# A polysketch attention and feed-forward kernel: the order of its steps behind the sixtieth, and who runs some of them

## The chip, the core and the metric

The kernel runs on one core of a Trainium2 chip. The metric is the device time of one execution in microseconds (us). The core's engines are TensorE (PE, the matmuls, with its weight loads PEld), VectorE (DVE), ScalarE (ACT), GpSimd (POOL) and SyncE (SP, which issues most of the transfers). Each runs its own instructions in the order of the program and waits for the others on semaphores.

## The reference

```python
{'batch': 4, 'n_heads': 4, 'seq': 1088, 'head_dim': 32}; r = 8
def phi(x):
    a = np.einsum('rd,bhsd->bhsr', S1, x)
    b = np.einsum('rd,bhsd->bhsr', S2, x)
    return np.einsum('bhsi,bhsj->bhsij', a, b).reshape(*x.shape[:-1], r * r)
q_p, k_p = phi(q), phi(k)
kv = np.einsum('bhsf,bhsd->bhfd', k_p, v)
z = np.sum(k_p, axis=2)
num = np.einsum('bhsf,bhfd->bhsd', q_p, kv)
den = np.einsum('bhsf,bhf->bhs', q_p, z)[..., None] + 1e-06
attn_out = num / den
x = attn_out.transpose(0, 2, 1, 3).reshape(4352, 128)
h = ((x @ w1) * (x @ w2)) @ w3        # w1, w2: 128 x 1024, w3: 1024 x 1024
out = h @ w_out                       # w_out: 1024 x 128
```

Linear attention with a feature map of 64 products a token, and then a feed-forward block in which two projections are multiplied. All inputs and the output are float32.

## The kernel before

The work is cut into some 1,700 named steps. The part ahead of the dot says of what: `k0` to `k3` and `q0` to `q6`, `qr` are the keys and queries of the attention by batch or chunk, `s` the sketch matrices, `w0` to `w10` pieces of the weights, `f` the products of w3 with w_out, `g0` to `g7` the feed-forward block for 512 tokens each, `gr` the same for the last 256 tokens, `h4` and `h6` a shared form for the groups g4/g5 and g6/g7 that makes two groups from seven products (`P1` to `P7`) of sums. The part behind the dot is the operation: `load` a transfer in, `gram` the 32-wide products of a key chunk with itself (line 659), `T` and `N` small products that build the sketch's coordinates (lines 883 to 912), `kv` the sums over keys (line 769), `x` the attention output (lines 1297, 1527), `a`, `b` (lines 1799, 1809) the two projections, `m` their product, `o` the output product (1824, 1835), `P` the output product of the shared form (1759), `k1` to `k9` the additions that build the two groups from the products (lines 1771 to 1785), `oT` the transposition of an output block, `oS` a scaling of it on POOL or DVE (1848), `st` its store (1556, 1562). A step `.a0` or `.a1` of a weight (line 470) adds the two halves of split weight words; `.c`, `.m`, `.j` (lines 263, 462, 466) come ahead of it.

The constants `zeros`, `ident` and masks come first. `ORDER` is one list of all steps; every engine runs its own instructions in the order in which the list has them. `SLOTS` is one string for each kind of buffer: which buffer the n-th user gets. The set `POOL` names the steps whose additions run on POOL and not on DVE, `CPV` and `CPG` the copies that run on DVE and on POOL and not on ACT. A step waits, through semaphores, for what it reads and for the buffer it writes. `WARM` gives the number of idle matmuls (line 255) in the steps `warm0` to `warm11`: they keep TensorE busy at the start and compute nothing that is used. The transfers of weights and of q, k, v are issued on SP in the order of the list, each only when the fourth before it has landed:

```python
WARM = [27, 2, 3, 4, 4, 4, 1, 2, 1, 1, 2, 2]
UNDER_WAY = 4
for ins, ahead in zip(bulk[UNDER_WAY:], bulk):
```

A matmul's weight tile has rows and columns, and its shape differs by step: 128 by 128 in `a`, `b`, `o`, 128 by 64 in `P`, 64 by 128 in the sums ahead of them (line 1673), 128 by 32 in `gram` and `kv`, 32 by 32 in `N` and the later `x`.

## Time and profile before

| what | us |
|---|---|
| median of three runs (lowest, highest) | 245.12 (245.04, 245.3) |
| the profiled execution, first to last instruction (its span) | 244.1 |
| the median above that span | 1.0 |
| TensorE matmuls, busy | 236.2 |
| DVE, busy | 206.7 |
| POOL, busy | 161.9 |
| ACT, busy | 123.5 |
| mean granted TensorE clock | 0.998 |

The profiled execution's own time is its span, and what lies around it before and behind is in the runs' times and not in the span. The first feed-forward product starts at 27.42 us; the last matmul ends at 240.57; the last store is issued at 240.95. "Issue" among the waits is time in which an engine waited for nothing that the profile shows.

### The profile page before, as it was taken

How to read it: one execution, taken by the hardware profiler on the slowest of the kernel's cores; microseconds unless marked ns; L12 is line 12 of the kernel's file. 1: busy time of each engine (PE TensorE's matmuls, PEld its weight loads, DVE VectorE, ACT ScalarE, POOL GpSimd, SP SyncE). 2: the span in 40 equal slices, each digit the busy share in tenths (PEclk: the TensorE clock that was granted, in tenths of full speed). 3: DMA queues.
4: the chain of work that ended last, by engine and by line, in shares of the span. 5: the costliest groups of instructions: out<-in, count | busy, mean ns of one | idle time of the engine just before them, and what ended most of it. 6: DMA issues, size and time to landing. Idle time of an engine off the chain costs nothing.

```text
span 244.1 us, 6745 instructions
## 1 busy us (share of the span) xinstructions
PE 236.2 (97%) x2724; PEld 129.8 (53%) x2724; DVE 206.7 (85%) x421; ACT 123.5 (51%) x246; POOL 161.9 (66%) x203
## 2 busy tenths in 40 slices
PE   8998999899999999999999999999999999999994
...
PEclk9999999999999999999999999999999999999999
...
GB/s 201 265 143 325 181 227 190 6 197 224 220 141 251 188 217 190 59 1 3 3 0 0 4 0 3 59 113 3 1 0 0 0 3 0 0 1 3 12 90 93
DMA packets 31935, 22.06 MB, mean 90 GB/s; under 512 B 21280, under 2 KB 26528, under 8 KB 31904
## 3 DMA queue, kind: packets, MB, share of 16 engines
...
q8 instruction: 21, 0.34, 0.6%
...
## 4 chain that ended last, share of the span: by engine, by line
PE 87%; DMA 5%; ACT 2%; POOL 2%; DVE 1%; issue 1%; POOLq 0%; SPq 0%
PE b_ps L1809 12%; PE ps_o L1835 12%; PE ps_X L1673 11%; PE a_ps L1799 11%; PE ps_o L1759 10%; PE ps_w3o L534 6%; PE ps_Y L1673 6%; PE ps_Z L1673 3%; PE ps_g L659 2%; PE ps_x L1527 2%; PE ps_ac L1374 2%; DMA qh<-in_q_dram 2%; DMA k<-in_k_dram 2%; PE ps_or L1824 2%; POOL ph L1208 1%; PE idle_ps L255 1%
## 5 line engine op out<-in xcount | busy, mean ns | idle before, releaser
L1673 PE MATMUL ps_X<-xd,wv 64*128 64x512 f32 x112 | 36.3, 593 | 0.0
L1799 PE MATMUL a_ps<-xT,w 128*128 128x512 f32 (+1 forms) x80 | 36.1, 562 | 0.0
L1809 PE MATMUL b_ps<-xT,w 128*128 128x512 f32 (+1 forms) x80 | 35.6, 555 | 0.0
L1804 ACT COPY ffa<-a_ps 128x512 f32<-128x512 f32 (+1 forms) x38 | 20.1, 540 | 29.2 <-PE a_ps L1799 26.7
L1707 POOL TENSOR_TENSOR hc<-hc 128x512 f32<-128x512 f32 x16 | 20.7, 1304 | 15.7 <-DVE hc L1685 15.5
L1835 PE MATMUL ps_o<-ab,w3o 128*128 128x512 f32 x64 | 29.6, 600 | 0.0
L1680 ACT COPY hc<-ps_X 128x512 f32<-128x512 f32 x38 | 21.3, 590 | 16.1 <-PE ps_X L1673 12.9
L1815 DVE TENSOR_TENSOR ab<-ffa,b_ps 128x512 f32<-128x512 f32 (+1 forms) x40 | 23.9, 623 | 4.9 <-PE b_ps L1809 4.1
L501 POOL TENSOR_TENSOR w3c<-w3c,cv_m 128x512 int32<-128x512 int32 x16 | 21.2, 1344 | 4.2 <-DVE w3c L495 4.1
L1673 PEld LDWEIGHTS ps_X<-xd,wv 64*128 64x128 f32 x112 | 14.9, 186 | 13.1 <-issue 10.9
L1799 PEld LDWEIGHTS a_ps<-xT,w 128*128 128x128 f32 x80 | 14.1, 189 | 13.9 <-issue 8.8
L1809 PEld LDWEIGHTS b_ps<-xT,w 128*128 128x128 f32 x80 | 14.4, 190 | 13.1 <-issue 8.1
L1673 PE MATMUL ps_Y<-xd,wv 64*128 64x512 f32 x48 | 19.7, 594 | 0.0
L1835 PEld LDWEIGHTS ps_o<-ab,w3o 128*128 128x128 f32 x64 | 11.6, 190 | 13.4 <-issue 13.0
L534 PEld LDWEIGHTS ps_w3o<-wo,w3T 128*128 128x128 f32 x128 | 15.3, 192 | 2.4 <-issue 2.4
L534 PE MATMUL ps_w3o<-wo,w3T 128*128 128x128 f32 x128 | 15.7, 276 | 0.0
L1759 PE MATMUL ps_o<-hc,w3o 128*64 128x512 f32 x32 | 15.1, 595 | 0.0
L1759 PE MATMUL ps_o<-tt,ws 128*64 128x512 f32 x32 | 13.7, 594 | 0.0
L1680 ACT COPY hc<-ps_Y 128x512 f32<-128x512 f32 x14 | 8.1, 592 | 9.7 <-PE ps_Y L1673 6.6
L263 ACT ACTIVATE cv_c<-raw 128x1024 f32<-128x1024 f32 (+1 forms) x13 | 13.0, 1014 | 0.0
L1540 ACT COPY xd<-ps_x 64x256 f32<-64x256 f32 x24 | 8.8, 367 | 7.2 <-PE ps_o L1835 6.8
...
## 6 DMA issues: line engine op xcount, KB each, us to landing
...
```

Of the source, the lines that this page charges most:

```text
L263: act.activation(dst, hi.bitcast(F32), ACT.Prelu, scale=2.0 ** -112, alpha=-2.0 ** 32)
L501: pool.tensor_tensor(d, d, x["m"][:, i * 512:(i + 1) * 512], ALU.add)
L534: pe.matmul(t["o"], w3T[ko][:, c], wo[:, c], start=c == 0, stop=c == NC - 1)
L1673: pe.matmul(x[bank], stat(j, u)[:, i * 128:(i + 1) * 128], rows(j, u), start=new, stop=True, tile_position=(u * 64, 0), skip_group_check=True)
L1680: cp(n(y))(x[k], x[bank])
L1707: on(f"h{g}.{i}m{k}").tensor_mul(both[0][k], both[0][k], both[1][k])
L1759: pe.matmul(acc_o[bank][half[0]:half[1]], w(i), x(i), start=n == 1, stop=n == (2 if j == 3 else 4), tile_position=(0, half[0]), skip_group ...
L1799: pe.matmul(x["a"][:, :w], w_of(0, c), xT[g][:, c0:c0 + w], start=True, stop=True)
L1804: cp(f"g{g}.{c}{su}c")(x["s"][:, :w], x["a"][:, :w])
L1809: pe.matmul(x["b"][:, :w], w_of(1, c), xT[g][:, c0:c0 + w], start=True, stop=True)
L1815: dve.tensor_mul(ab_sb[g, c][:, c0:c0 + w], x["s"][:, :w], x["b"][:, :w])
L1835: pe.matmul(o_ps[g], w3o[:, c], ab_sb[g, c], start=n == 1, stop=n == NC)
```

## The change

The instructions are the same, and the first 60 steps of the list stay. Behind them `ORDER` is another list of the same steps. With it the buffers in `SLOTS` change, and the engine of some steps: TensorTensor instructions on DVE are 189 instead of 201 and on POOL 143 instead of 131, copies on ACT 168 instead of 173 and on DVE 26 instead of 21. `WARM` is the same, but `warm8`, `warm9` and `warm11` stand elsewhere in the list.

```diff
 POOL = set("""
-    g4.oS g5.oS g6.oS g7.oS h4.0T1 h4.0T2 h4.0T3 h4.0m12 h4.0m22 h4.1T2 h4.1m11 h4.1m12 h4.2m11
...
+    g5.oS g6.oS g7.oS h4.0T2 h4.0T3 h4.0m11 h4.0m12 h4.0m22 h4.1T1 h4.1T2 h4.1T3 h4.1m11 h4.1m12
...
 ORDER = """
...
-k1.zero s.Pm warm5 q0.l1 q0.A0 warm6 kr0.ab k0.lead1 q0.rm q0.sma q0.sta warm7 k0.kT0 v0.load v0.loadr k1.load k0.ab1
...
-k0.Gm k0.Gt k0.Ga w1.c1 k0.Gb k0.abc0 k0.T0 q1.l1 warm8 kr0.abc k0.kp1 q0.sca w1.j1 k0.Ta k0.kp0 k0.Gc w1.c0 k1.tr0
-kr1.load k2.zero k1.tr1 k1.kT1 kr0.kp warm9 k0.N0 warm10 k0.Na warm11 k0.T1 k0.kv0 k0.Tc k0.Tb k0.N1 k0.Nb k0.Nh q1.rm
...
-k0.kvm w1.m0 kr1.kT q0.p01 q1.C0 q1.C1 q0.C1 k0.kzt k2.loadr q0.pt0 q0.C1t q0.scy q0.p2 k0.kz q0.pt1 k0.kvc kr1.ab
-k0.kqt q0.p12 q0.dn q0.de q0.rc w1.j0 q0.pc0 q0.pc1 q0.x0 k1.kT0 q0.x1 q0.xs0 q0.xs1 q0.xt0 w1.a0 q1.A0 k2.load
-w0.load k1.lead0 q0.xc0 q0.xc1 k0.kq w1.a1 k2.max q0.xt1 k1.ab q0.xT0 q0.xT1 g0.4a q1.load g0.5a q1.sm w0.m1 q1.st
...
-q1.pc0 q1.pt1 g0.1b w9.load k1.N0 s.AR q2.l1 q2.rm v3.zero q1.pc1 k1.N1 q1.x g0.6c g0.1c k1.Na k1.Nr k3.zero k2.gram0
-g0.1m k2.gram1 k2.gram2 q3.max k2.gram3 g0.0c k2.kT0 k1.Nb q1.xT k2.gram4 q3.l2 k2.ab q2.A0 q2.C0 q2.C1 q3.l1 k1.kp0
...
-h6.1P2 h6.3P6 h6.2m12 h6.2T4 h6.3T4 h6.2P7 h6.2P6 h6.3P4 h6.2P4 g4.oT h6.2P2 gr.3o1 h6.k1 gr.2o0 gr.2o1 h6.2P3 h6.k3
-g4.oS h6.k2 h6.k4 h6.0P3 gr.7o0 g4.st gr.0a gr.5b h6.k5 h6.k6 h6.3P3 h6.1P3 h6.k7 g5.oS q6.ns gr.4a gr.3o0 gr.4b gr.0c
-gr.4c gr.1b gr.0b g6.oT gr.6a h6.k8 g5.st h6.k9 g7.oT gr.7o1 gr.6b gr.6c gr.0m gr.0o1 gr.4m gr.4o1 gr.0o0 gr.4o0 gr.5m
-gr.5o0 g6.oS g6.st g7.oS g7.st gr.6m gr.6o1 gr.1m gr.6o0 gr.1o0 gr.5o1 gr.oT0 gr.1o1 gr.oT1 gr.st1
+k1.zero s.Pm warm5 q0.l1 q0.A0 warm6 kr0.ab k0.lead1 q0.rm q0.sma k0.kT0 k0.ab1 kr1.load warm10 k0.ab0 k0.rest1
...
+k1.lead0 q0.sly k0.kv2 k0.kvr q1.C1 s.KS q0.C1t q0.phi1 q0.p01 q0.scy k0.kvc q0.p2 w9.load q0.pt0 q0.p12 q1.Ct w1.j0
+k0.kvm q0.dn q1.sh q0.pt1 q0.de kr1.abc q1.sl k0.kzt q0.pc0 w0.load k0.kqt q1.sca k0.kz k2.zero w1.a0 q0.pc1 q0.rc
+q0.x0 q0.xs0 w1.j1 k2.load q0.xs1 q0.x1 q0.xc0 q0.xt0 q2.tr q0.xc1 w0.m1 q0.xt1 k1.ab q0.xT0 q0.xT1 w1.a1 q1.p01
...
+k2.loadr q1.restT kh2.load k1.gram1 k1.gram2 w0.j1 q1.p12 s.AR k1.gram3 q1.dn k1.gram4 k1.abt q1.de q1.rc k1.Gm w0.a1
...
+q2.l1 k2.lead0 g0.0c w0.a0 k2.rest0 k2.kT1 q1.pt0 k2.gram0 k1.Gc k2.gram1 k2.kT0 g0.4m k1.Gb k1.T0 k2.gram2 k2.gram3
+w9.c k3.zero g0.2c k2.gram4 g0.3c k1.T1 k1.Ta k2.Gm w9.m w9.j w5.load q1.pc0 q3.l1 k1.Tb k1.Tc g0.7b q1.pc1 q3.rm
+g0.1a warm8 g0.7m g0.1c k2.Gt g0.1b g0.6b k3.load g0.1m k1.N0 q2.rm k1.kp0 v1.zero w2.c k1.Na k1.Nr q1.x k1.N1 k2.ab
...
+h6.k1 gr.3m h6.1P4 h6.2P6 h6.3P5 h6.3T3 h6.1P6 h6.3P7 h6.2T4 h6.3P2 h6.0P7 h6.3P6 q6.ns g4.oS h6.3P3 h6.3T4 g4.st
+h6.0T4 h6.k2 h6.k3 h6.2P4 h6.0P3 h6.0P4 h6.1P3 h6.3P4 h6.k4 h6.k7 gr.2o0 gr.7o1 h6.k5 gr.6a h6.k6 gr.6c h6.k8 gr.0b
+gr.1b gr.3o1 g6.oT g6.oS gr.6b gr.4a gr.0m gr.7o0 gr.4c h6.k9 g7.oT gr.4b gr.0o1 gr.0o0 g6.st gr.4m g7.oS gr.2o1
+gr.5o1 gr.4o1 gr.4o0 gr.6m gr.1m gr.6o1 gr.3o0 g7.st gr.6o0 gr.5o0 gr.1o1 gr.1o0 gr.oT0 gr.oT1 gr.st1
...
```

These are the lines of the diff that hold the steps spoken of below; the others differ in the same way. The places of interest are shown by each engine's instructions in program order. (A row is a line of the kernel, the instruction, output <- inputs, the size of the output, and how many in a row; the lines of the changed kernel are one higher.)

**TensorE at the gram products of k2** (`ps_g`; a matmul `kk` and one `k,kk` alternate; `ps_ph` transposes features of q1, `ps_N` and `ps_T` are k1's, `ps_x` is q1's attention output). Before, what stands ahead of them:

```order
L1799 MATMUL a_ps<-xT,w_81 128x512 x2
L1809 MATMUL b_ps<-xT,w_81 128x512
L1246 MATMUL ps_ph<-ident,ph 128x128 x4
L1809 MATMUL b_ps<-xT,w_81 128x512
L912 MATMUL ps_N<-T_p,P2a 32x8 x4
L912 MATMUL ps_N<-T_p,P2b 32x8 x4
L912 MATMUL ps_N<-T_p,P2s 32x8 x8
L1297 MATMUL ps_x<-pT,kz_605 64x512 x2
L659 MATMUL ps_g<-kk 32x64
L659 MATMUL ps_g<-k,kk 32x32
```

Now, the end of them and what follows:

```order
L660 MATMUL ps_g<-kk 32x64
L660 MATMUL ps_g<-k,kk 32x32
L890 MATMUL ps_T<-RS,G_a 32x32
L891 MATMUL ps_T<-RS,G_c 32x32
L892 MATMUL ps_T<-RS,G_b 32x32
L1810 MATMUL b_ps<-xT,w_81 128x512
L1800 MATMUL a_ps<-xT,w_81 128x512
L256 LDWEIGHTS zeros
L256 MATMUL idle_ps<-zeros 128x256
L1810 MATMUL b_ps<-xT,w_81 128x512 x2
L913 MATMUL ps_N<-T_p,P2a 32x8 x4
L1298 MATMUL ps_x<-pT,kz_646 64x512 x2
```

Before, `ps_N` and `ps_x` stand directly ahead of the gram products and k2's next products directly behind them; now k1's `ps_T` is in and behind them, and the feed-forward steps `g0.7b`, `g0.1a`, `g0.1b`, `g0.6b` with the idle step `warm8` come ahead of `ps_N` and `ps_x`.

**POOL ahead of the additions of w1** (`w_81` x2 is `w1.a0` and `w1.a1`; `s_` are steps of q0 and q1). Before:

```order
L1170 TENSOR_TENSOR s_al<-s_hla 128x128
L949 TENSOR_TENSOR RS<-RC,mask_65 128x64
L1208 TENSOR_TENSOR ph<-s_al,s_bs 128x512
L386 TENSOR_TENSOR KS<-Sc,mask_67 128x32
L1176 TENSOR_TENSOR s_pr<-s_hla,s_hiy 128x256
L470 TENSOR_TENSOR w_81<-w_81,cv_m 128x2x256 x2
L378 COPY RC<-Sc 128x4x8 x3
L1161 TENSOR_TENSOR s_hl<-s_hl,ay_C 128x128
```

Now:

```order
L1209 TENSOR_TENSOR ph<-s_al,s_bs 128x512
L950 TENSOR_TENSOR RS<-RC,mask_65 128x64
L387 TENSOR_TENSOR KS<-Sc,mask_67 128x32
L1177 TENSOR_TENSOR s_pr<-s_hla,s_hiy 128x256
L1102 TENSOR_TENSOR s_loy<-s_loy,ay_C_595 128x128
L1181 TENSOR_TENSOR s_pr<-s_al,s_loy 128x128
L1185 TENSOR_TENSOR s_pr<-s_pr 128x128
L1162 TENSOR_TENSOR s_hl<-s_hl,ay_C 128x128
L557 MEMSET k 64x4x32
L471 TENSOR_TENSOR w_81<-w_81,cv_m 128x2x256 x2
L1177 TENSOR_TENSOR s_pr<-s_hl 128x256
```

`q0.phi0` is on POOL and `q0.phi1` on DVE; q0's `scy`, `p2`, `p12`, q1's `sca` and a memset of a key buffer stand ahead of the two additions, and the copy `RC` stands behind them.

**The tail** (`ps_o` are the products `h6.P`, `ps_or` the outputs of gr, `a_ps` and `b_ps` its projections). TensorE before:

```order
L1759 MATMUL ps_o<-tt,w3o 64x512 x2
L1759 MATMUL ps_o<-hc,w3o 64x512
L1824 MATMUL ps_or<-w3o,ab 128x128 x3
L1759 MATMUL ps_o<-hc,ws 64x512 x2
L1824 MATMUL ps_or<-w3o,ab 128x128
L1799 MATMUL a_ps<-xT,w_81 128x256
L1809 MATMUL b_ps<-xT,w_81 128x256
L1759 MATMUL ps_o<-hc,ws 64x512 x2
L1799 MATMUL a_ps<-xT,w_81 128x256
L1824 MATMUL ps_or<-w3o,ab 128x128
L1809 MATMUL b_ps<-xT,w_81 128x256 x3
```

TensorE now:

```order
L1760 MATMUL ps_o<-tt,w3o 64x512
L1760 MATMUL ps_o<-hc,ws 64x512
L1760 MATMUL ps_o<-tt,w3o 64x512
L1825 MATMUL ps_or<-w3o,ab 128x128 x2
L1800 MATMUL a_ps<-xT,w_81 128x256
L1810 MATMUL b_ps<-xT,w_81 128x256 x2
L1825 MATMUL ps_or<-w3o,ab 128x128
L1810 MATMUL b_ps<-xT,w_81 128x256
L1800 MATMUL a_ps<-xT,w_81 128x256
L1825 MATMUL ps_or<-w3o,ab 128x128
L1810 MATMUL b_ps<-xT,w_81 128x256
```

DVE before (lines 1776 to 1785 are `h6.k2` to `h6.k9`, the two transpositions `g6.oT` and `g7.oT`):

```order
L1779 TENSOR_TENSOR oc<-oc,ps_o 64x512
L1776 TENSOR_TENSOR oc<-oc,ps_o 64x512
L1780 TENSOR_TENSOR oc<-oc,ps_o 64x512
L1781 TENSOR_TENSOR oc<-oc,ps_o 64x512
L1782 TENSOR_TENSOR oc<-oc,ps_o 64x512
L1783 TENSOR_TENSOR oc<-oc,ps_o 64x512
L1842 STREAM_TRANSPOSE oT<-oc 128x512
L1784 TENSOR_TENSOR oc<-oc,ps_o 64x512
L1785 TENSOR_TENSOR oc<-oc,ps_o 64x512
L1842 STREAM_TRANSPOSE oT<-oc 128x512
```

DVE now:

```order
L1777 TENSOR_TENSOR oc<-oc,ps_o 64x512
L1780 TENSOR_TENSOR oc<-oc,ps_o 64x512
L1781 TENSOR_TENSOR oc<-oc,ps_o 64x512
L1784 TENSOR_TENSOR oc<-oc,ps_o 64x512
L1782 TENSOR_TENSOR oc<-oc,ps_o 64x512
L1783 TENSOR_TENSOR oc<-oc,ps_o 64x512
L1785 TENSOR_TENSOR oc<-oc,ps_o 64x512
L1843 STREAM_TRANSPOSE oT<-oc 128x512
L1816 TENSOR_TENSOR ab<-ffa,b_ps 128x256
L1786 TENSOR_TENSOR oc<-oc,ps_o 64x512
L1843 STREAM_TRANSPOSE oT<-oc 128x512
```

The products of h6 stand together, with the steps of gr behind them (the last three of the `ps_o` rows end the run of 28; `h6.3P6` is the 22nd of it), and `h6.k8` comes ahead of `g6.oT`. SP issues the four stores of g6, the four of g7 and the last one of gr behind these, as before.

More of the change, by code (lines that the diff above doesn't have):

```diff
@@ L88 @@
-q1.sca q2.tr g0.5c q1.al q1.p01 q1.p2 k1.gram2 k1.gram3 kr1.abc k1.gram4 w6.load w0.m0 g0.6b w0.j0 g0.7c g0.7m k1.Gm
-q1.p12 k1.Gc g0.0a w2.load w0.a1 q1.dn q1.de q1.rc q1.bs k1.Gt g0.3a k1.Ga k1.T0 k2.kT1 k1.Gb g0.3c q1.restT g0.2a
-q1.phi k1.T1 q1.pt0 g0.4m w0.a0 q2.max q2.l2 g0.6a k1.Ta k2.lead0 k2.rest0 g0.1a g0.2c k1.Tc g0.5b q3.tr g0.5m k1.Tb
-q1.pc0 q1.pt1 g0.1b w9.load k1.N0 s.AR q2.l1 q2.rm v3.zero q1.pc1 k1.N1 q1.x g0.6c g0.1c k1.Na k1.Nr k3.zero k2.gram0
-g0.1m k2.gram1 k2.gram2 q3.max k2.gram3 g0.0c k2.kT0 k1.Nb q1.xT k2.gram4 q3.l2 k2.ab q2.A0 q2.C0 q2.C1 q3.l1 k1.kp0
```

142 lines of the change are left out of this document (73 added, 69 removed).

## The prediction

> **What bounds the kernel now.** I read the page first, then the busy time by stretches, the waits of TensorE, and the chain of work in the places that the change touches. From the page (engine totals; TensorE's busy tenths and granted clock in forty slices; instruction transfers; the chain's share by engine):
>
> ```profile
> PE 236.2 (97%) x2724; PEld 129.8 (53%) x2724; DVE 206.7 (85%) x421; ACT 123.5 (51%) x246; POOL 161.9 (66%) x203
> PE   8998999899999999999999999999999999999994
> PEclk9999999999999999999999999999999999999999
> q8 instruction: 21, 0.34, 0.6%
> PE 87%; DMA 5%; ACT 2%; POOL 2%; DVE 1%; issue 1%; POOLq 0%; SPq 0%
> ```
>
> TensorE is busy for 236.2 of 244.1 us and holds 87% of the chain. Its matmuls stay the same, so time can come only from its gaps, from what a matmul costs beside its neighbours, and from the two ends of the program. The stretches (PE, PEld, DVE, ACT, POOL busy, clock, DMA share, GB/s) say where gaps are:
>
> ```profile
> 20.00:30.00 10.00, 9.31 (x167) 6.28 (x167) 8.15 (x23) 7.90 (x18) 6.05 (x9) 1.00 0.80 229
> 30.00:40.00 10.00, 9.76 (x172) 5.03 (x171) 8.54 (x24) 7.07 (x18) 6.78 (x7) 1.00 0.90 215
> 40.00:50.00 10.00, 8.84 (x280) 5.24 (x279) 8.91 (x23) 5.42 (x10) 5.47 (x7) 1.00 0.23 59
> 60.00:220.00 160.00, 160.00 (x1490) 83.16 (x1489) 141.42 (x254) 79.05 (x154) 118.18 (x106) 1.00 0.25 57
> 230.00:240.00 10.00, 10.00 (x59) 6.75 (x56) 8.59 (x15) 1.12 (x3) 6.63 (x21) 1.00 0.51 86
> ```
>
> From 60 to 220 us there is no gap; the one large gap behind 30 us lies between 40 and 50, where only 59 GB/s are moved. TensorE's waits name it:
>
> ```profile
> PE ps_g L659 <- issue: 1.6, 2, 1.2
> PE idle_ps L255 <- DVE zeros L229: 1.0, 1, 1.0
> PE ps_kv L769 <- issue: 0.9, 1, 0.9
> ```
>
> "Issue" means that nothing in the profile held TensorE. The three such gaps are at `k0.gram3` (about 14 us), `k0.kv3` (19 us) and `k2.gram3` (46 us). I counted TensorE's stream, every weight load and every matmul as one: the instructions behind the gaps are numbers 452, 708 and 1732, and 452 + 256 = 708, 708 + 4 x 256 = 1732. The page has 21 transfers of instructions, 0.34 MB / 21 = 16 KB each, for 2 x 2724 = 5448 instructions, and 5448 / 256 = 21.3. So the gaps are the places where a new page of 256 instructions had not come yet. The chain at the first and around the third:
>
> ```profile
> 13.86 0.41 issue
> 14.27 0.58 PE ps_g L659 x23
> ...
> 42.90 0.36 PE ps_N L912 x32
> 43.26 1.01 PE ps_x L1297 x4
> 44.27 1.56 PE ps_g L659 x75
> 45.83 1.16 issue
> 46.98 0.54 PE ps_g L659 x15
> ```
>
> Between 43.2 and 47.0 us TensorE ran through one whole page in 3.8 us, 1.16 of them the gap; a page lasts 244 / 21.3 = 11.5 us on average. Many small matmuls in a row (a load and a matmul every 0.02 us) outrun the fetch.
>
> **The page stall: -1.2 us.** In the new order the k2.gram run is broken up: the T products of k1, four feed-forward steps (`g0.7b g0.1a g0.1b g0.6b`) and an idle one now stand in and behind it in the same page. With 0.86 us a step (below) that page holds about 1.5 (four gram steps) + 3.6 + 1 (the rest) = 6 us of work, longer than the 3.8 it took with its gap. The gap of 1.16 should go: -1.2 us with the loss just beside it. Bounds: -1.4 (the page counts from the first late load) and 0 (the gap turns up at another boundary, as `k0.kv3` had one of 0.9 us in the stretch where loads are busy). I take -1.2, since DMA is light here. The two early gaps, 0.6 and 0.9 us, lie where TensorE waits for other engines anyway; I give them nothing.
>
> [...]
>
> **Changes of tile shape: -1.05 us.** What a step costs when the rows and columns of the weight tile differ from the step before:
>
> ```profile
> 57.61 0.86 PE a_ps L1799 x2
> 59.84 1.05 PE a_ps L1799 x2
> 230.93 0.87 PE ps_or L1824 x6
> 231.79 1.01 PE ps_o L1759 x4
> 232.80 0.42 PE ps_or L1824 x2
> 235.09 0.63 PE a_ps L1799 x2
> 235.72 0.22 PE ps_or L1824 x2
> ```
>
> An a step of 512 columns is 0.86 us behind its like and 1.05 behind the 32-column T products: 0.19 more. In the tail three `ps_or` steps cost 0.87 where 3 x 0.22 = 0.66 is due (0.21 more), one costs 0.42 (0.20 more), two output products (128x64) 1.01 where 2 x 0.43 = 0.86 is due (0.15 more), an a step 0.63 instead of 0.43 (0.20). So a change costs 0.15 to 0.2 us. Counted along the two orders from the first feed-forward step on, there are 54 changes before and 48 now. Four of the six are in the tail, where the excursions `gr.3o1 gr.2o0 gr.2o1` and `gr.7o0 gr.0a gr.5b` no longer stand among the h6 products. 6 x 0.175 = 1.05 us, bounds 0.6 (the early ones hidden) and 1.2.
>
> **Idle matmuls: +0.44 us.** Four of them (`warm8`, `warm9`, two of `warm11`) stood where TensorE had time before 18 us and now stand behind 30 us, where each costs what this row says:
>
> ```profile
> 17.15 0.11 PE idle_ps L255
> ```
>
> 4 x 0.11 = 0.44, nothing to cover it; bounds 0.3 and 0.5.
>
> **The first feed-forward steps: +0.4 us.** They need the weight words of w1, added on POOL (`w1.a0`, `w1.a1`, line 470). Before (timeline; the last column is the idle time ahead):
>
> ```profile
> 25.94 2.51 POOL L470 TENSOR_TENSOR w<-w,cv_m 128x512 int32<-128x512 int32 x2 [3.63 <-DVE w L466]
> 27.42 1.96 PE L1799 MATMUL a_ps<-xT,w 128*128 128x512 f32 x4
> 18.62 0.46 POOL L1170 TENSOR_TENSOR s_al<-s_hla 128x128 f32<-128x128 f32 x1
> 29.43 1.50 POOL L1161 TENSOR_TENSOR s_hl<-s_hl,ay_C 128x128 f32<-128x128 f32 x1 [0.33 <-DVE s_hl L1157]
> ```
>
> POOL was idle for 3.63 us ahead of the additions. Now `q0.scy`, `q0.p2`, `q0.p12`, `q1.sca` and a memset stand ahead of them: 4 x 0.46 + 0.2 = 2.0 us, which the idle time holds, unless `q1.sca` is late: it waits for q1's split into a rounded part and the rest on DVE. The first two steps (`g0.5b`, `g0.7a`) read different halves of w1, so the second waits for the second addition: 1.26 (half of 2.51) against 0.86 of work, +0.4 us. Before, the first three steps read the first half, and this was covered. How far the first step itself moves no row tells: q0's products come in much the same order, q1's partly ahead of them. I take nothing for it, so +0.4, with bounds of -0.1 (the start 0.5 earlier) and +1.7 (a late `q1.sca`, priced under the rivals).
>
> Sum for TensorE's last matmul: -1.2 - 1.05 + 0.44 + 0.4 = -1.4 us.
>
> **The tail: +0.9 us.** Chain and queue at the end of before (the SP rows are issues, the POOL one the last addition to a block of output):
>
> ```profile
> 238.33 2.25 PE ps_or L1824 x20
> 240.60 0.29 DVE oT L1858
> 236.40 1.96 SPq L1556 DMA_DIRECT2D out_dram<-oT  x4
> 238.58 2.01 SPq L1556 DMA_DIRECT2D out_dram<-oT  x4
> 240.95 0.62 SPq L1562 DMA_DIRECT2D out_dram<-oT  x1
> 231.69 0.69 DVE L1780 TENSOR_TENSOR oc<-oc,ps_o 64x512 f32<-64x512 f32 x1
> 236.65 0.71 DVE L1842 STREAM_TRANSPOSE oT<-oc 128x512 f32<-128x512 f32 x1
> 235.32 1.05 POOL L1848 TENSOR_TENSOR oT<-oT,nz 128x512 f32<-128x512 f32 x1
> ```
>
> The last matmul ends at 240.57, the last store is issued 0.38 later, and 3.1 us behind that the span ends. SP is free at 240.6: the eight stores of g6 and g7, 0.5 us each, just fit. In the new order `h6.k3` waits for `h6.3P6`, the 22nd of 28 products; behind it on TensorE are 6 products (6 x 0.43) and 22 `gr` steps (6 x 0.43 + 16 x 0.22 = 6.1, and 0.2 for the change of shape). So `k3` can start 8.9 us ahead of the last matmul's end E. Then DVE runs `k3 k4 k7 k5 k6 k8` and g6.oT (before, `k8` came behind g6.oT): 6 x 0.69 + 0.71 = 4.9, POOL takes 1.05, and some 0.2 lie between the steps: the stores can go out at E - 2.8. Eight of them take 4.0 and a little, so the last store is issued at E + 1.3 where before it was E + 0.38: +0.9 us. Bounds: 0 (DVE gets ahead) and +1.5 (`gr.0m` and other work slips in between). What was covered by 0.35 us of slack on SP is the bound now.
>
> Whole sum against the profiled span: 244.1 - 1.4 + 0.9 = 243.6 us. The median of the runs, 245.12, is 1.0 above the span of 244.1 (what lies around it, taken as unchanged), so 244.6.
>
> **The rivals.**
> *The store queue doesn't bind.* If DVE runs `k2` and `k7` early enough, the whole 1.4 us arrives: 245.1 - 1.4 = 243.7. For it: in 230 to 240 DVE has 1.4 us free. Against: the six additions form one chain.
> *POOL holds the start (slower).* Place: `q1.sca` on POOL, straight ahead of the w1 additions; it cannot start before q1's split on DVE is done, and no row of before says when that will be. The one such step in the trace took 1.50 us, its like at 18.62 only 0.46. If it starts at 25.5 and takes 1.50, it ends at 27.0, the memset at 27.2, the first addition at 28.5 instead of 27.2 (25.94 + 1.26), and TensorE loses 1.3 us at the first step and 0.4 at the second: 1.7 in all. With -1.81 for the three other terms and +0.9 for the tail that is 245.1 + 0.8 = 245.9. It decides from a loss of 1.4 us on (0.91 to be back at 245.1, and 0.49): from a start at 25.2, at that length. For it: TensorE has nothing else there. Against: at 0.46 us the same start costs 0.7 in all, and POOL's idle time holds the rest.
> *Loads come late (slower).* SP now issues w9 (1 MB) ahead of w0: at 229 GB/s that is 4.6 us later for w0, wanted by the sixth step, some 6 us after the first. If that lacks 1.5 us, the time is 245.1 - 1.8 + 0.9 + 0.4 + 1.5 = 246.1.
> *Nothing comes of it.* The gap of 1.16 us turns up at another page boundary again: 244.6 + 1.2 = 245.8 at most, 245.2 with half of it.
>
> **How the numbers follow.** A difference of 0.2%, 0.49 us, is about what a measurement of this kernel can tell from none: faster is below 244.63, slower above 245.61. The forecast case has 0.46 (its own range 244.2 to 245.1, 0.27 of it on the faster side), the free store queue 0.15, POOL at the start 0.16, late loads 0.09, nothing 0.14 (0.11 within the bound). Faster: 0.27 + 0.15 = 0.42. Slower: 0.16 + 0.09 + 0.03 = 0.28. Same: 0.19 + 0.11 = 0.30. The range for 8 in 10 takes in the free queue and the slow cases at their prices: 243.5 to 246.3.
>
> **What would show it.** TensorE's waits: "issue" at `ps_g` falls from two to one or none, and none is longer than 0.3 us behind 27 us. The stretch 40 to 50 shows TensorE busy near 10.00. The h6 products end in one run of 28 (about 12 us), and the tail has single `ps_or` steps of 0.22. On SP the eight stores go out with no pause, and the last one over 1 us behind the last matmul. It is wrong if TensorE's first feed-forward step starts later than 28 us, if waits for POOL `w` or for loads stand among TensorE's waits with over 1 us, or if new gaps of "issue" appear.

## The result: 5.6% slower

| | before | the change |
|---|---|---|
| median, us (lowest, highest; six runs each, same chip) | 245.21 (244.93, 245.91) | 258.62 (258.02, 260.18) |
| ratio, 95% interval | | 1.0559 [1.0527, 1.0591] |
| span of the profiled execution, us | 244.1 | 257.9 |
| first feed-forward product starts, us | 27.42 | 31.70 |
| last matmul ends, us | 240.57 | 253.46 |

Medians are of all runs; ratios leave disturbed executions out, so that one can differ from the ratio of its medians. The change costs 13.4 us; the prediction was 244.6, and its range ended at 246.3. The page of the profile after (engine totals, TensorE's busy tenths and granted clock in forty slices, the chain's shares):

```profile
PE 245.2 (95%) x2724; PEld 141.7 (55%) x2724; DVE 220.6 (86%) x414; ACT 119.9 (46%) x241; POOL 169.9 (66%) x215
PE   8988888999999979999999999999999999999993
PEclk9995999999999999999999999999999999999998
PE 70%; DVE 19%; issue 4%; ACT 3%; POOL 2%; DVEq 0%; POOLq 0%; ACTq 0%
```

TensorE has the same 2724 matmuls and is busy 9 us longer. DVE held 1% of the chain before and holds 19% now, and DVE's own busy time has grown by 13.9 us. The waits of TensorE after the change:

```profile
PE ps_g L660 <- DVE kk L652: 1.5, 1, 1.5
PE ps_x L1528 <- DVE pT L1518: 1.5, 1, 1.5
PE a_ps L1800 <- POOL w L471: 1.2, 1, 1.2
PE b_ps L1810 <- POOL w L471: 0.4, 1, 0.4
PE ps_g L660 <- issue: 0.2, 1, 0.2
```

The large gap of "issue" at `k2.gram3` is gone, as forecast. In its place TensorE waits for work of DVE and POOL. Two of the three signs of being wrong that the prediction names are there: the first feed-forward step starts behind 28 us, and TensorE waits over 1 us for POOL's `w`. By stretches (columns as in the prediction):

```profile
20.00:27.00 7.00, 6.44 (x139) 5.53 (x139) 3.50 (x12) 4.33 (x9) 3.89 (x7) 0.51 1.00 270
27.00:40.00 13.00, 10.96 (x213) 6.18 (x211) 10.99 (x25) 10.45 (x26) 8.80 (x11) 1.00 0.78 193
40.00:50.00 10.00, 8.46 (x175) 5.17 (x174) 9.20 (x19) 5.61 (x11) 7.34 (x8) 1.00 0.81 189
160.00:200.00 40.00, 39.76 (x224) 22.36 (x226) 35.79 (x54) 20.61 (x46) 28.85 (x23) 1.00 0.13 22
200.00:246.00 46.00, 45.95 (x203) 22.65 (x200) 43.11 (x64) 15.45 (x30) 38.04 (x55) 1.00 0.07 12
```

From 20 to 27 the granted clock is 0.51 (1.00 before). From 27 to 40 TensorE is busy 10.96 of 13 us, where it was 12.76.

**Where the time went.** I set the start of each step on TensorE beside its start before. The first feed-forward product is 4.3 us later. The step that waits for the second addition of w1 loses 1.5 more, `k2.gram0` 2.1 at its wait for DVE, and the page gap gives 1.4 back. q3's attention output (`ps_x` behind `pT`) loses about 1.8, the steps of h4 and h6 from 163 us on lose 5.0, and the end behind the last matmul 0.9. That is 14.2 for a span that grew by 13.8; the rest of the program gives some 0.4 back.

**The start.** DVE's chain at 13 us, here DVE's row and then the two POOL rows beside it (timelines after the change):

```profile
13.60 2.53 DVE L205 SCALAR_TENSOR_TENSOR s_hla<-s_ga,s_t 128x128 f32<-128x128 f32 x1
```

```profile
13.45 0.62 POOL L841 TENSOR_TENSOR kpr<-krab 128x256 f32<-128x256 f32 x1
14.03 1.94 POOL L678 TENSOR_TENSOR kp<-kab 128x1024 f32<-128x1024 f32 x1
```

This is `q0.sha`, which took 0.29 at 11.64 before and stood ahead of POOL's product `kp`:

```profile
11.64 0.29 DVE L204 SCALAR_TENSOR_TENSOR s_hla<-s_ga,s_t 128x128 f32<-128x128 f32 x1
```

Now it starts beside `kpr` and ends 0.16 us behind the end of `kp` (15.97). What stands behind it in DVE's queue has to wait for it. The chain of waits at the first feed-forward products shows what ends last there:

```profile
29.37 0.07 POOL s_hl L1162
...
30.38 3.63 POOL w L471 x2
34.05 1.98 PE a_ps L1800 x4
```

`q1.sca` (L1162) runs at 29.37, behind a DVE step, and the two additions of w1 start at 30.38. They take 3.63 together where they took 2.51, because DVE runs `k1.rest0` (1.70; the longest such step on DVE before took 1.35) beside the second.

**k2 and q3.** The wait at `k2.gram0` is for `k2.rest0`, which takes 2.33 us on DVE beside POOL's `w0.a0`; a step of this form took 1.35 before. The wait at q3's attention output goes back through DVE's queue to `w6.j`, DVE's row and then POOL's:

```profile
86.70 2.42 DVE L496 TENSOR_SCALAR w3c<-cv_c 128x1024 int32<-128x1024 int32 x1
```

```profile
86.61 1.96 POOL L1510 TENSOR_TENSOR ph<-s_al,s_bs 128x1024 f32<-128x1024 f32 x1
```

The other steps of its form take 0.67 to 0.69 at the median, so 1.7 us of the 1.8 that are lost there can come from this step alone. It reads one operand from SBUF, not two.

**The h4 and h6 sums.** DVE in the change from 196 us on, then POOL at the same time:

```profile
196.31 1.76 DVE L1743 TENSOR_TENSOR tt<-tt,hc 128x512 f32<-128x512 f32 x1
197.99 1.75 DVE L1728 TENSOR_TENSOR tt<-hc 128x512 f32<-128x512 f32 x1
199.66 0.68 DVE L1708 TENSOR_TENSOR hc<-hc 128x512 f32<-128x512 f32 x1
200.26 1.76 DVE L1738 TENSOR_TENSOR hc<-hc 128x512 f32<-128x512 f32 x1
```

```profile
195.80 1.72 POOL L1708 TENSOR_TENSOR hc<-hc 128x512 f32<-128x512 f32 x1
197.48 1.72 POOL L1743 TENSOR_TENSOR tt<-tt,hc 128x512 f32<-128x512 f32 x1
199.88 1.59 POOL L1733 TENSOR_TENSOR tt<-hc,tt 128x512 f32<-128x512 f32 x1 [0.69 <-DVE tt L1728]
```

Each of the three long DVE additions ends 0.54 to 0.55 us behind the end of the POOL addition that it met (197.52, 199.20, 201.47); the one at 199.66, which starts while POOL is idle, takes 0.68. The POOL additions pay too: the second starts at 197.48 beside a DVE step that ends at 198.07, and ends 1.13 later. In the same block before the change, DVE and POOL:

```profile
182.32 0.68 DVE L1742 TENSOR_TENSOR tt<-tt,hc 128x512 f32<-128x512 f32 x1
```

```profile
181.62 8.77 POOL L1497 COPY nz<-nz 32x8 f32<-32x8 f32 x16
```

There POOL had 16 small copies to do while DVE ran its chain of sums, and all additions of that chain took 0.68 to 0.69. The copies pay: they take 8.77 here and 4.64 in the change, where they stand beside additions from PSUM. Over the whole kernel, DVE's steps above the usual length of their form add up to 8 to 9 us before and 20 to 22 after; some 6.6 of the 12 us more lie behind 160 us.

The loss in this block can't be seen as idle TensorE. The rows of TensorE's largest group from 60 us on, before and after:

```profile
L1673 PE MATMUL ps_X<-xd,wv 64*128 64x512 f32 x112 | 36.3, 593 | 0.0
```

```profile
L1674 PE MATMUL ps_X<-xd,wv 64*128 64x512 f32 x112 | 38.5, 604 | 0.2 <-ACT xd L1541 0.2
```

One such matmul is shown about 600 ns long, while the next may start 0.21 us behind it, so a pause of less than some 0.4 us shows as busy time. The same 112 matmuls are busy 2.2 us longer.

**The tail.** The chain at the end, and SP's last stores:

```profile
233.72 13.22 PE ps_o L1760 x56
...
250.62 2.80 PE ps_or L1825 x24
```

```profile
250.45 4.18 SPq L1557 DMA_DIRECT2D out_dram<-oT  x8
254.74 0.62 SPq L1563 DMA_DIRECT2D out_dram<-oT  x1
```

The last store is issued 1.3 us behind the last matmul, by eight stores with no pause between them: the term of the tail, to the tenth. The 28 h6 products come in one run, but in 13.22 us and not in 12.0.

### The profile page after: what moved, and what is told of

The parts are those of the page before. It is cut to its first block, busy times and chain, and to the rows that moved or that the text cites. A ratio compares the mean times of both kernels' runs of the same rounds, so it can differ in the third digit from the quotient of the medians.

```text
span 257.9 us, 6763 instructions
## 1 busy us (share of the span) xinstructions
PE 245.2 (95%) x2724; PEld 141.7 (55%) x2724; DVE 220.6 (86%) x414; ACT 119.9 (46%) x241; POOL 169.9 (66%) x215
## 4 chain that ended last, share of the span: by engine, by line
PE 70%; DVE 19%; issue 4%; ACT 3%; POOL 2%; DVEq 0%; POOLq 0%; ACTq 0%
PE ps_X L1674 10%; PE ps_o L1836 10%; PE a_ps L1800 8%; PE b_ps L1810 8%; PE ps_o L1760 5%; PE ps_w3o L535 5%; PE ps_Y L1674 5%; PE ps_Z L1674 3%; PE idle_ps L256 3%; DVE ab L1816 3%; ACT xd L1541 2%; PE ps_ac L1375 2%; PE ps_kv L770 2%; PE ps_x L1528 2%; PE ps_or L1825 2%
## 5 line engine op out<-in xcount | busy, mean ns | idle before, releaser
L1674 PE MATMUL ps_X<-xd,wv 64*128 64x512 f32 x112 | 38.5, 604 | 0.2 <-ACT xd L1541 0.2
L1810 PE MATMUL b_ps<-xT,w 128*128 128x512 f32 (+1 forms) x80 | 36.5, 557 | 0.4 <-POOL w L471 0.4
L1708 POOL TENSOR_TENSOR hc<-hc 128x512 f32<-128x512 f32 x18 | 24.9, 1391 | 12.1 <-DVE hc L1686 12.0
L1805 ACT COPY ffa<-a_ps 128x512 f32<-128x512 f32 (+1 forms) x33 | 17.2, 536 | 26.9 <-PE a_ps L1800 26.8
L1681 ACT COPY hc<-ps_X 128x512 f32<-128x512 f32 x35 | 19.9, 590 | 17.5 <-PE ps_X L1674 13.1
L502 POOL TENSOR_TENSOR w3c<-w3c,cv_m 128x512 int32<-128x512 int32 x16 | 22.6, 1423 | 8.1 <-DVE w3c L496 6.7
L1674 PEld LDWEIGHTS ps_X<-xd,wv 64*128 64x128 f32 x112 | 16.0, 186 | 10.9 <-issue 5.4
L1674 PE MATMUL ps_Y<-xd,wv 64*128 64x512 f32 x48 | 21.6, 599 | 0.0
L1760 PE MATMUL ps_o<-hc,ws 128*64 128x512 f32 x32 | 14.1, 596 | 0.0
L485 ACT ACTIVATE cv_m<-raw 128x1024 int32<-128x1024 uint32 x9 | 10.6, 1179 | 4.9 <-DVE w3T L529 3.5
```

What stands on the lines that cost most here:

```text
L502: pool.tensor_tensor(d, d, x["m"][:, i * 512:(i + 1) * 512], ALU.add)
L1674: pe.matmul(x[bank], stat(j, u)[:, i * 128:(i + 1) * 128], rows(j, u), start=new, stop=True, tile_position=(u * 64, 0), skip_group_check=True)
L1681: cp(n(y))(x[k], x[bank])
L1708: on(f"h{g}.{i}m{k}").tensor_mul(both[0][k], both[0][k], both[1][k])
L1760: pe.matmul(acc_o[bank][half[0]:half[1]], w(i), x(i), start=n == 1, stop=n == (2 if j == 3 else 4), tile_position=(0, half[0]), skip_group ...
L1805: cp(f"g{g}.{c}{su}c")(x["s"][:, :w], x["a"][:, :w])
```

## The experiments

My theory after the two traces: DVE steps with two operands in SBUF stand still beside POOL, and the new order brings more of them together; at the start the late `q0.sha`, the halved clock and the late `k2.rest0` add to it. The rivals: the new order is bad in one piece only, the buffers do it, or DVE has too much work.

### Halves of the order

Each of the first four kernels takes a part of the list of steps from one order and the rest from the other, with the engines that the steps of a part have there, and gives each buffer to the user for whom it has been free longest. `early_only` has the first 182 steps of the new list (of 1,179; the "some 1,700" further up is too many), `early_as_before` its reverse, `late_as_before` the new list up to `h4.s1` and then the old one, `middle_only` the old list at both ends.

```diff
 ORDER = """
...
-k1.zero s.Pm warm5 q0.l1 q0.A0 warm6 kr0.ab k0.lead1 q0.rm q0.sma q0.sta warm7 k0.kT0 v0.load v0.loadr k1.load k0.ab1
+k1.zero s.Pm warm5 q0.l1 q0.A0 warm6 kr0.ab k0.lead1 q0.rm q0.sma k0.kT0 k0.ab1 kr1.load warm10 k0.ab0 k0.rest1
...
```

> The first 182 steps (to k1.ab, just ahead of the first feed-forward product) in the new order with the new engines; all others as before. Buffers handed out anew, longest free first. If the loss is made before the first product (it starts at 31.7 us in the changed kernel, 27.4 before, and 1.5 more go at the w1 additions), 249 to 251 us. If the early part only exposes what comes later, under 246.5.

> The first 178 steps (to k1.ab) as before, all others in the new order with the new engines. If losses of the parts add up: 258.6 less 4.3 to 5.8, so 252.8 to 254.3 us. If a late start is absorbed later on, 257 or more.

> The new order and engines up to h4.s1 (the sums ahead of the products of h4), all behind it as before. In the changed kernel TensorE's steps of h4 and h6 take 4.9 us more than before, and the tail 1.1. If DVE and POOL additions that meet each other in that part make this, 258.6 - 6 = 252.6 us. If these steps are late only because what feeds them is late, 257 or more.

> Early part (to k1.ab) and late part (from h4.s1) as before, only the middle in the new order. If the losses add up: 245.2 and the middle's own 2 to 3 us, so 247 to 248.5 us. If the middle is what is dear, over 252.

Measured against before: `early_only` 253.42, ratio 1.031 [1.022, 1.039]; `early_as_before` 261.91, 1.065 [1.058, 1.073]; `late_as_before` 259.68, 1.056 [1.038, 1.074]; `middle_only` 257.10, 1.046 [1.035, 1.056]. No loss came out as the sum of its parts would have it: `early_only` is over both of its ranges, and the other three lie in the open ranges written down for the other case (257 or more, 257 or more, over 252). Putting the old start back made the change slower, not faster, and three kernels that each have only a part of the change lose 8, 14 and 11 us. Losses of parts that each come near to the whole don't add up to it: either the mixing itself costs, or each part needs the other. A run for that alone keeps before's order and engines and only gives the buffers to the longest free:

```diff
 SLOTS = {
     "b":
-        "012345670214657210671306537457462512346127340273014526045721472352140327540542370673245716"
...
+        "012345670245672140624306723156731542731426730264705432671453704015437061537315067206153240"
...
```

> The kernel before, same order and engines, with all buffers handed out anew, longest free first, as in the four runs that mix the two orders. If the choice of buffers took no part in those: 245 to 246 us. If it did, 248 or more, and the mixed runs say little about the order.

It takes 252.35, ratio 1.0312 [1.0258, 1.0365]. Buffers alone cost 7 us:

```profile
PE a_ps L1791 <- DVE s_hl L196: 1.5, 1, 1.5
PE ps_kv L761 <- POOL kp L669: 1.1, 1, 1.1
PE b_ps L1801 <- ACT hc L1672: 0.8, 1, 0.8
```

The four mixed runs carry this cost and say little on the order. The kernels below keep the buffers of the kernel that they start from, but for those that a moved step forces (fewer than ten, but about 150 of kind `b` where the idle matmuls move, and 40 to 50 of kind `m` with the spare steps below).

### The start: q0.sha, the idle matmuls, k2.rest0

`after_sha_early` takes the change and puts q0's `sta` and `sha` back ahead of the key products. `after_idle_back` puts `warm8`, `warm9` and `warm11` back to about where they stood before, behind `k0.gram4`, `kr1.tr` and `k0.N1`, with 5, 6 and 8 idle matmuls where they had 1, 1 and 2. `after_rest_on_pool` gives `k2.rest0` back to POOL. `after_sha_and_idle` does the first two.

```diff
-q0.rm q0.sma k0.kT0
+q0.rm q0.sma q0.sta q0.sha k0.kT0
```

```diff
-WARM = [27, 2, 3, 4, 4, 4, 1, 2, 1, 1, 2, 2]
+WARM = [27, 2, 3, 4, 4, 4, 1, 2, 5, 6, 2, 8]
...
-k0.gram4 q0.sla
+k0.gram4 warm8 q0.sla
...
```

> The changed kernel with the DVE steps q0.sta and q0.sha (lines 202 and 205) moved up to directly behind q0.sma, as before, so that they run ahead of POOL's k0.kp1 (1.95 us) and not beside it; nothing else. Theory A (a DVE step with two operands in SBUF stands still while POOL works on two operands in SBUF: q0.sha took 2.53 us here instead of 0.29, everything behind it came 2.2 us late, TensorE ran dry between 15 and 20 us, and its clock fell to half from 20.5 to 26.5): q0.sha takes under 0.5 us, the clock stays, the first feed-forward product starts 3 to 4 us earlier (28 to 29 us), and the time is 254 to 256 us. Rival B (the missing idle matmuls let the clock fall, whatever DVE does): the clock still falls, and the time is over 257.

> The changed kernel with warm8, warm9 and warm11 put back into the early part (behind k0.gram4, kr1.tr and k0.N1), with 5, 6 and 8 idle matmuls in place of 1, 1 and 2, so that TensorE is busy while it waits there. Theory B (clock alone): the granted clock stays at 1.00 between 20 and 27 us, the first product starts 3 us earlier, the time is 254 to 256 us. Theory A (late work, the clock is a smaller part of it): the clock stays, but the first product starts at most 1.5 us earlier, and the time is 256.5 to 258.5.

> The changed kernel with k2.rest0 (line 652) on POOL again, as before, where it met POOL's w0.a0 as a DVE step and took 2.33 us instead of 1.35, and TensorE waited 1.5 us for it at k2.gram0. Theory A: it takes 2.6 us on POOL, queued behind w0.a0, so TensorE waits as long or longer there: the time is 258 to 260 us (a step can't be saved from meeting by changing its engine when the other engine is busy). Rival C (DVE is the overloaded engine and any step taken from it helps): 256.5 us or less.

> Both edits of the early part in one: q0.sta and q0.sha directly behind q0.sma, and warm8, warm9, warm11 back in the early part with 5, 6 and 8 idle matmuls. Alone they gave 256.8 and 257.2 us; in the first the clock fell later (28.6 to 35 us), in the second the chain behind q0.sha stayed late. If these two causes hold the whole early loss: the clock stays at 1.00, the first feed-forward product starts near 28 us, and the time is 253 to 254.5 us. If the additions of w1 on POOL hold it by themselves, 255.5 to 257.

| kernel | us | ratio to before |
|---|---|---|
| the change | 258.62 | 1.0559 [1.0527, 1.0591] |
| `after_sha_early` | 256.76 | 1.0497 [1.0438, 1.0556] |
| `after_idle_back` | 257.16 | 1.0472 [1.0424, 1.0521] |
| `after_sha_and_idle` | 256.92 | 1.0476 [1.0428, 1.0525] |
| `after_rest_on_pool` (255.91, 257.76, 261.19, 262.97; the ratio is of the first two) | 259.47 | 1.0472 [1.0423, 1.0521] |

With `q0.sha` early, q1's product `q1.C1` ends 4.1 us earlier and the first feed-forward product starts 3.3 earlier, but 1.9 arrive, less than the 254 to 256 of my theory. In the profiled execution the clock falls later instead (0.50 from 29 to 35 us); that is not what takes the rest, for two others with a mean clock of 0.997 and 0.999 took 256.53 and 256.75, and this one 256.77 (the fourth, with 0.984, took 259.74).

With the idle matmuls back the clock stays at 1.00 in the profiled execution (0.991, 0.999 and 0.993 in the others) and 1.5 us arrive, in the range for late work. What brings them is open: 15 idle matmuls are new, and so are about 150 buffers. The clock hardly does, for the change itself took 258.86 in the execution with a mean clock of 1.000, and 258.02 to 260.18 in the five with 0.982 to 0.991.

The two together bring no more than one. 256.92 lies in the range that was written down for the additions of w1, but the trace shows another hold: the first feed-forward product starts at 30.16, behind q0's attention output on DVE (`q0.xT1`), and the first of these additions is done at 29.88. Before that, TensorE stands still for 1.5 us and waits for nothing that the profile shows. The same gap in `after_idle_back`:

```profile
PE ps_kz L781 <- issue: 1.3, 1, 1.3
```

In both, the instruction behind it is about number 964 of TensorE's stream (weight loads, matmuls and waits counted), two times 256 behind the gap at `k0.gram3` (452). So a gap of the kind that was forecast to go has turned up at another boundary.

The trace of `after_rest_on_pool` is of its longest execution. There TensorE waits longer at `k2.gram0`, since `k2.rest0` queues behind `w0.a0` on POOL:

```profile
PE ps_g L660 <- POOL kk L652: 2.8, 1, 2.8
```

The two shorter executions, 255.91 and 257.76, are no slower than the change and lie around the rival's bound of 256.5, so that this run decides nothing.

None of these edits brings more than some 2 us, and the interval of `after_sha_early` overlaps that of the change; where the traces show what comes next, it stands close behind. `before_without_idle` is before without the four idle matmuls of these three steps; it leaves out nothing else:

```diff
-WARM = [27, 2, 3, 4, 4, 4, 1, 2, 1, 1, 2, 2]
+WARM = [27, 2, 3, 4, 4, 4, 1, 2, 0, 0, 2, 0]
```

> The kernel before with warm8, warm9 and warm11 set to no idle matmuls at all (four fewer, between 16 and 18 us). Theory B: the granted clock falls behind 20 us as in the changed kernel, the time is 247 us or more. Theory A: TensorE has enough work there without them, the clock stays at 1.00, the time is within 0.3 us of before.

245.05, ratio 0.999 [0.996, 1.002], clock 1.00: no difference.

### Do POOL and DVE hold each other up?

Two kernels put one extra step into before's order, which changes no result: a memset and six additions of a tile to itself on POOL. `two_spare_beside_sums` has it beside DVE's chain of h4 sums, with `q4.ns` (the small copies) moved behind `h6.s4`; `two_spare_apart` has it behind `h6.s4`, where DVE adds operands from PSUM.

```diff
+    @step("spare")
+    def _():
+        t = sb("oc", [128, 512])
+        pool.memset(t, 0.0)
+        for _ in range(6):
+            pool.tensor_add(t, t, t)
...
-h4.2P7 q4.ns h4.2P6
+h4.2P7 spare h4.2P6
```

> The kernel before with extra work on POOL: one memset and six additions (128x512, two operands in SBUF, of zeros; nothing reads them), put where DVE adds the h4 products' halves with two operands in SBUF (181 to 191 us in before), and the small copies q4.ns behind h6.s4. Alone each takes POOL 1.27 us. Theory A (a DVE addition of two SBUF operands stands still while POOL does the same): each of the six meetings costs DVE 1 us, the DVE additions there go from 0.68 to 1.7 us, and the time rises by 2 to 5 us, to 247.5 to 250.5. Rival D (POOL's load or what waits for POOL is dear, not the meeting): no DVE addition there gets longer, and the time is that of the twin run, in which the same work stands elsewhere.

> The same memset and six additions on POOL, but behind h6.s4 (192 to 200 us in before), where DVE adds with one operand in PSUM. Theory A: DVE's additions stay at 0.69 us, POOL was idle there for 7.8 us, so the time is 245.0 to 246.0. Rival D: as slow as the twin run.

Beside the sums: 249.0, ratio 1.0165 [1.0129, 1.0202]. Apart: 245.23, 1.001 [0.9988, 1.0033]. DVE and POOL beside the sums:

```profile
184.34 0.68 DVE L1710 TENSOR_TENSOR hc<-hc,ps_X 128x512 f32<-128x512 f32 x1
185.79 1.52 DVE L1725 TENSOR_TENSOR tt<-hc 128x512 f32<-128x512 f32 x1
188.69 1.52 DVE L1735 TENSOR_TENSOR hc<-hc 128x512 f32<-128x512 f32 x1
190.13 1.52 DVE L1705 TENSOR_TENSOR hc<-hc 128x512 f32<-128x512 f32 x1
```

```profile
184.15 8.40 POOL L227 TENSOR_TENSOR spare<-spare 128x512 f32<-128x512 f32 x6
```

The same, apart:

```profile
192.40 0.68 DVE L1774 TENSOR_TENSOR oc<-oc,ps_o 64x512 f32<-64x512 f32 x1 [0.45 <-PE ps_o L1757]
```

```profile
191.90 6.62 POOL L227 TENSOR_TENSOR spare<-spare 128x512 f32<-128x512 f32 x6
```

The same POOL work costs 3.8 us at one place and nothing at the other. A DVE addition with one operand in PSUM takes 0.68 in both; with both in SBUF it takes 1.52 beside POOL. One ACT copy (`h6.0ae`) waited for the spare tile's buffer in the first kernel and ran at 192.58 instead of 184.50, but no large wait of TensorE is for it, and the chain there goes through DVE's stretched steps, 184.9 to 194.8. What the meetings cost is shown: 4.3 us on DVE in the six of them, and 1.1 more in a seventh (`h4.3T4`, 1.76, beside `h6.s4`, which the spare steps pushed there on POOL); 3.8 of these 5.4 arrive in the time.

The cure would be fewer meetings. `after_halves_on_dve` gives the sixteen h4 and h6 sums that run on POOL to DVE:

```diff
 POOL = set("""
-    g5.oS g6.oS g7.oS h4.0T2 h4.0T3 h4.0m11 h4.0m12 h4.0m22 h4.1T1 h4.1T2 h4.1T3 h4.1m11 h4.1m12
+    g5.oS g6.oS g7.oS h4.0m11 h4.0m12 h4.0m22 h4.1m11 h4.1m12
...
```

> The changed kernel with the 16 steps h4.xTy and h6.xTy that it has on POOL (1.27 us each) put on DVE (0.68 us each). DVE gets 10.9 us more to do. Theory A: ten meetings of 1.0 us on DVE and 0.4 us on POOL go, so that this costs nothing or gains: 256.5 to 259 us, and DVE's longest addition behind 190 us falls from 1.76 to under 1.0 us. Rival (DVE's load is the limit there): 262 to 268 us.

262.76, ratio 1.0713 [1.0673, 1.0754]: the rival was right. The stretch of DVE's steps from 180 to 200 us falls from 3.1 to 0.2, but the sixteen additions now stand in DVE's own queue, and TensorE waits longer for DVE behind `h4.1P5` (1.9 us to the next product) and `h6.0P6` (2.3). Not every meeting is gone: `h6.1T2` still takes 1.76 us at 235. This fits DVE as the bound of this block, with no slack to take a meeting; a kernel that has the sums of the change without the meetings was not run.

### The terms of the sum, one at a time

`before_gram_apart` takes before and puts `g0.5b g0.5m` behind `k2.gram1` and `g0.1b g0.1m` behind `k2.gram2`, as the change does with its steps. `before_one_step_in_page` does it with `g0.1b` alone.

```diff
-k3.zero k2.gram0 g0.1m k2.gram1 k2.gram2 q3.max k2.gram3
+k3.zero k2.gram0 k2.gram1 g0.5b g0.5m k2.gram2 g0.1b g0.1m q3.max k2.gram3
```

> The kernel before with g0.5b and g0.5m put behind k2.gram1, and g0.1b and g0.1m behind k2.gram2, so that two feed-forward steps of 0.86 us lie in the page of instructions that TensorE outran; a few buffers differ. By the prediction's term the gap of 1.16 us at k2.gram3 goes: 243.9 to 244.4 us. If the page is not what is waited for there, the gap stays and the time is 245.1 to 245.7.

> The kernel before with one step only, g0.1b, put behind k2.gram1, and its product g0.1m behind k2.gram4, so that DVE does k2.kT0 and k1.Nb first. The gap at k2.gram3 shrinks by the 0.86 us of the step. If DVE is not held by it this time: 244.2 to 244.8 us. If the wait for DVE's kabt comes back as with two steps, 245.6 or more.

247.74, ratio 1.0108 [1.0081, 1.0135], and 245.33, 1.0011 [0.9993, 1.0028]. In both the gap at `k2.gram3` is gone: the step took 1.74 us and takes 0.50 and 0.52, that is 1.24 and 1.22 less. Neither kernel is faster. With two steps moved, this comes in place of the gap:

```profile
PE ps_ab L718 <- DVE RC L927: 1.1, 1, 1.1
PE a_ps L1790 <- DVE kabt L736: 1.1, 1, 1.1
```

The second of these waits goes back to a meeting that the move brought: `k1.kp0` takes 2.27 us on DVE beside POOL's `k1.kp1`, where it took 1.22. With one step moved, TensorE is done with `q1.pt1` before DVE is done with `k1.Tb`, and waits:

```profile
PE ps_N L903 <- DVE T_p L895: 0.4, 1, 0.4
```

The moved step covered that wait; among the gram products it takes 1.06 us and not 0.86. Of the 1.22 us, 0.3 are left from `q1.pt1` to `k2.ab`, and the time shows nothing of them. (This trace is 0.6 us late already at `q1.pt0`: its gap at `k0.gram3` is 1.42 us, where that of before is 0.41. These early gaps differ between kernels that are the same up to there.)

`before_tail_together` puts the excursions `gr.3o1 gr.2o0 gr.2o1 gr.7o0 gr.0a gr.5b` behind the last h6 product, as the change does, and so takes four changes of tile shape out of the tail.

```diff
-h6.2P2 gr.3o1 h6.k1 gr.2o0 gr.2o1 h6.2P3
+h6.2P2 h6.k1 h6.2P3
...
-h6.3P3 h6.1P3 h6.k7
+h6.3P3 h6.1P3 gr.3o1 gr.2o0 gr.2o1 gr.7o0 gr.0a gr.5b h6.k7
```

> The kernel before with gr.3o1, gr.2o0, gr.2o1, gr.7o0, gr.0a and gr.5b put behind the last product of h6, so that the 28 products stand together as in the changed kernel; a few buffers differ. By the prediction four changes of tile shape go, 0.7 us, and DVE's additions start earlier, so that the stores still fit: 244.4 to 244.8 us. If a change of shape costs nothing on the path, or the tail is held by the stores, 245.1 to 245.7.

From the first h6 product to the start of `gr.7o1`, TensorE takes 16.41 us instead of 17.10: 0.69 less, and 0.70 by the prediction's price of 0.175. DVE's chain of h6 additions ends when it did before (236.6 us), so that the products of gr behind it wait, and the last matmul ends 0.26 earlier, at 240.30. The time is 245.36, ratio 1.0009 [0.9992, 1.0026]: no gain that a measurement shows. More than about 0.4 could hardly have come, because SP's sixteen stores ahead of the last one end at 240.5 to 240.6 in both kernels, and the last one was issued at 240.95.

### Order, engines and buffers apart

`after_old_engines` has the change's order and buffers with before's choice of engines for additions and copies; `before_new_engines` the reverse.

```diff
 POOL = set("""
-    g5.oS g6.oS g7.oS h4.0T2 h4.0T3 h4.0m11 h4.0m12 h4.0m22 h4.1T1 h4.1T2 h4.1T3 h4.1m11 h4.1m12
+    g4.oS g5.oS g6.oS g7.oS h4.0T1 h4.0T2 h4.0T3 h4.0m12 h4.0m22 h4.1T2 h4.1m11 h4.1m12 h4.2m11
...
```

> The changed kernel (new order, new buffers) with the sets POOL and CPV of the kernel before, so that only the order and the buffers are new. If the new choice of engines made the meetings and with them the loss: 250 us or less. If order and engines fit each other only as a pair (meetings depend on what stands beside what): 258 us or more.

> The kernel before (old order, old buffers) with the sets POOL and CPV of the changed kernel. If the new choice of engines is what costs: 250 us or more, with more DVE additions over 1.0 us than before. If the order is what costs: 245 to 248 us.

267.69, ratio 1.0936 [1.0877, 1.0995], and 282.99, 1.1559 [1.1495, 1.1623]. The largest waits of TensorE in the second:

```profile
PE ps_w3o L535 <- DVE w3T L529: 4.3, 1, 4.3
PE ps_o L1760 <- POOL tt L1743: 3.3, 1, 3.3
```

Both lie in the slow one of their ranges, and together they speak for the pair: with the old choice of engines the new order loses 9 us more, and the new choice on the old order costs 38. In these two swaps each list fits its own order and not the other, so the 13 us can't be divided among them by swapping. None of these kernels beats before.

## Why the prediction was wrong

**The step that failed** is the one under all the others: the sum was made of changes on TensorE and the durations of DVE and POOL steps were carried over from the rows of before. I read "from 60 to 220 there is no gap" as TensorE being the bound with DVE's 88% of busy time (141.42 of 160) behind it, and took for granted that the same instructions in another order would feed it as well. They don't: in the change a DVE addition of 128x512 lasts 0.68 or up to 1.76 us by what POOL does beside it. The rows of before held a sign of this. The prediction quoted a 128x128 addition on POOL of 0.46 and one of 1.50, and took the long one for a late step's bad luck, a price of one rival, instead of asking what stretched it: it ran at 29.43, beside DVE's `k1.rest0` (29.26 to 30.61). The chains of waits in the change lead to steps stretched in this way at each of the four large losses: `q0.sha` (2.53 for 0.29) and `w1.a1` (2.39 for 1.27) at the start, `k2.rest0`, `w6.j`, and the sums of h4 and h6. That 12 us more of stretch on DVE, which was near to full, make most of the 13.4 is my reading of these chains; no run that took a stretch away gained more than some 2 us.

**The page stall, -1.2 us: right in the trace, worth nothing in the time.** The gap went, and two kernels that removed it by moving one or two steps measured 1.22 and 1.24 us less at its place with no gain at the end. The step that failed is "the gap of 1.16 should go: -1.2 us with the loss just beside it". It named no work as due next; the waits for `kk`, `kabt`, `RC` and at `k1.N0` were within about a microsecond of it.

That the gaps belong to pages of 256 is a reading of counts. With the waits counted too, the trace of before has the instructions behind its three gaps at numbers 451, 706 and 1730, within two of the prediction's and 255 and 1,024 apart; weight loads and matmuls alone, as the prediction describes its count, give 444, 692 and 1702. The one gap of "issue" over 0.3 us that TensorE has in the change, 0.35 at 23.21 us, stands at 707.

**Changes of tile shape, -1.05 us:** the price was right. Four of the changes alone were worth 0.69 us on TensorE's steps, 0.17 each where I took 0.175. What failed is that it would reach the end: 0.26 of it came as far as the last matmul, because DVE's additions set when the steps behind them can run.

**Idle matmuls, +0.44 us:** too small beside the rest to be seen. The prediction did not ask what they did where they stood. In the profiled execution TensorE is less busy at the start without them and the clock is halved for 6.8 us, but an execution with a mean clock of 1.000 was no faster (258.86), so that the halved clock is not what made the loss. 19 idle matmuls in the old places went with 1.5 us; the cause of these is open. Before's order doesn't need them (0.999 without).

**The first feed-forward steps, +0.4 us:** mis-sized. The step that failed is "I take nothing for it": the first product came 4.3 us later, after a wait of 0.42, and the second after a wait of 1.22, 1.5 us more. The rival of POOL at the start had the place and the waiting step right (`q1.sca` ahead of the w1 additions), but 29.37 where it said 25.5, since it allowed for no delay of q0's own chain ahead of it: that `q0.sha` fell behind two POOL products was in the order, and I read only the w1 rows. With `q0.sha` early, `q1.sca` starts at 26.07. The other rival, late loads, did not show: none of TensorE's large waits is for a load.

**The tail, +0.9 us:** right. The last store is issued 1.3 us behind the last matmul, as worked out, at the end of eight stores with no pause.

**What stays open.** How the 5 us of the h4 and h6 block divide between meetings of DVE and POOL and the order of its sums is not settled; the spare steps show the price of a meeting, and the run that took the meetings away added load in the same move. The shares of order, engines and buffers are not settled either.
